# Attention scores of the first four blocks in banks of their own, and a table of held steps in the planner

## The chip, the cores and the metric

The kernel runs on one core of a Trainium2 chip. The metric is the time of one execution on the device, in microseconds (us); less is better. A core has five engines that run side by side, each through its own instructions in a fixed order: TensorE (PE, matrix products; the loads of its stationary operand are listed as PEld), VectorE (DVE), ScalarE (ACT), GpSimd (POOL) and SyncE (SP). They wait for each other by semaphores. Data come from main memory by DMA transfers, which SP, ACT and POOL issue. Products of PE land in PSUM, which has 8 banks, each 512 fp32 columns wide on 128 partitions; ACT and DVE read them from there.

## The reference

Sliding-window attention with four sink positions, then a gated feed-forward network (FFN):

```python
# q, k, v: 4 x 8 x 768 x 64 fp32; n_sink = 4, window = 128
scores = scale * np.matmul(q, k.transpose(0, 1, 3, 2))
is_sink = pos[None, :] < int(n_sink)
rel = pos[:, None] - pos[None, :]
keep = is_sink | ((rel >= 0) & (rel < int(window)))
scores = np.where(keep, scores, -1000000000.0)
a = softmax(scores)                       # over the keys
attn_out = np.matmul(a, v)                # -> x: 3072 x 512
rms = np.sqrt(np.mean(x * x, axis=-1, keepdims=True) + 1e-06)
xn = x / rms * rms_g
g = xn @ w_gate                           # 512 x 1536
out = (g * (1.0 / (1.0 + np.exp(-g))) * (xn @ w_val)) @ w_out
```

(The softmax is written out in the original.)

## The kernel before

**Blocks and groups.** The 3072 tokens are 24 blocks of 128, numbered `g`; 6 blocks make a batch `b`, and `t` is the place of a block in its batch. Four blocks make a group `G` of the FFN, six groups in all. As the window is 128 wide, the keys of block `g` are seen by the queries of blocks `g` and `g+1` alone; the sinks of a batch are handled apart (`ss`, `esk`, `vsk`).

**One block of attention.** q, k and v of a block are loaded (`load_bf16`, `load_v`, cast on the way from fp32 to bf16; block 0's q and k come as fp32 through SP with `load_f32` and are cast by DVE or ACT, `cast`). PE transposes q and k of blocks 0 to 7 (`pe_t`, L425), and DVE or ACT copies them out of PSUM (`copy_t`, L432). `scores` (L465) multiplies the keys of a block with the queries of this block and the next: for each of 4 head pairs and 2 halves, into the four banks `("s", g, u, hi)`. In a bank lie two heads, each with 256 columns: 128 for query block `g` (n = 0) and 128 for `g+1` (n = 1). ACT takes the exponential (`exps`, L513), bank by bank, into `e`. The window is cut either beforehand, by matmuls that put a bias into the banks (`mask_bias`, L447, blocks below `PE_MASKS` = 2), or afterwards by DVE (`mask_dve`, L530) or POOL (`mask_pool`, L535, from block `POOL_MASK_FROM` = 16). `av` (L549 to L566) multiplies with v, and needs the exponentials of block `g` for its own queries and those of block `g-1` for its next. Then DVE divides by the sums (`normal`, L577, L578), ACT squares (`square`, L586), DVE scales (`rms`, L593 to L610), and x is transposed, on PE below block 8 (`pe_x`, L625, `copy_x`, L631), else by DMA.

For blocks in `SPLIT` = (0, 1) the scores and exponentials run in two passes over the same four banks, first the 128 columns of n = 0 in each half, then those of n = 1. The others do both at once. So the scores of block 3 wait for q of block 4. In the last block of a batch there is no next query block: `scores_last` (L481) fills two banks. With `MERGE` = (2,) batch 2's last scores go into one PE step with the first of the next batch, and take six banks together.

**The FFN.** For each group `ffn` makes pairs of a gate product `g` and a value product `v` (`mms`, L860), 16, 8 or 8 matmuls a piece; ACT takes `tanh` (L867), DVE makes `silu` (L873) and `hidden` (L883), `project` (L893) multiplies with `wo`, ACT scales the result and SP stores it. `CHUNKS` = (4, 2, 2) cuts group 0 into four columns of one block each, with four f-tiles (128 columns of wg or wv) in one product: gate product (0, 0, 0) is that of f-tiles 0 to 3 on block 0.

**The order.** Each step is given to `Plan` with an estimated duration, what it needs and gives, a priority, and the banks it takes and drops. `Plan.run` simulates the engines: among all steps that could be next it takes the one with the smallest `(start, priority, ...)`, and the result is the order in which the program is emitted. On the chip, semaphores alone set the times; the plan sets who stands behind whom in an engine's queue. While PE would be idle, the plan places `warm` matmuls (L400, 30 of them) on zeros.

**The loads.** POOL issues the loads of `LOADS` in that order (`sw_load`, at most `DEPTH` = 8 of them under way in the plan): `q-1` is q of block 1, `qkv-2` is q, k and v of block 2, `w-2-4` is f-tiles 2 and 3 of wg and then of wv (L378), `wo-0-6` half of wo (L384). Before the first load POOL could make the identity (`make_ident`, L271) and the bias mask (`make_bias`, L277); `POOL_AT` places them behind q-1 and k-1.

**Gates.** From block `GATE_FROM` = 8 on, `gate_of` holds the scores of a block back until the FFN has come to a certain unit (a value product or a projection), `GATE_LEAD` = 14 units ahead of the block's place.

Of the kernel before, what the change touches and what calls it, by code (L numbers as in the profile page):

```python
# [26 lines left out]
class Plan:  # L27
# [2 lines left out]

    LATE = 300
    RESERVE = 8
    HOP = {"PE": 40, "ACT": 35, "DVE": 35, "POOL": 90, "SP": 60}
    START = {"PE": 800, "ACT": 800, "DVE": 1030, "POOL": 1290, "SP": 800}

# [5 lines left out]
    def op(self, ways, needs=(), gives=(), prio=0.0, takes=(), drops=(), ring=None, work=0.0,  # L43
           mode=0):
        self.ops.append(dict(
            ways=ways, needs=set(needs), gives=tuple(gives), prio=prio, takes=tuple(takes),
            drops=tuple(drops), ring=ring, work=work, mode=mode, at=len(self.ops), ready=0,
        ))

    def land(self, ring, first, work):  # L50
# [19 lines left out]
    def run(self):  # L70
# [12 lines left out]
        while left:  # L83
            first = None

            many = min(
                (o for o in cand["PE"] if len(o["takes"]) > self.RESERVE), default=None,
                key=lambda o: o["prio"],
            )
            for e, found in cand.items():  # L90
                for o in found:
                    k = len(o["takes"])
                    if k > len(self.banks):
                        continue
# [51 lines left out]
def kernel(  # L146
# [53 lines left out]
    GB_PRIO = -100000.0  # L200
    FUSE_FROM = 2
# [125 lines left out]
    def cast(name, g, copy):  # L327
        T[name, g] = ld.tile([P, H, D], BF16, name=name)
        copy(out=T[name, g], in_=T.pop(("st", name, g)))

    def load_bf16(name, src, g):
        T[name, g] = ld.tile([P, H, D], BF16, name=name)
# [10 lines left out]
    for i, name in enumerate(F32_LOADS):  # L343
        n, g, e = name[0], int(name[2:]), {"s": "SP", "a": "ACT"}[name[1]]
        src, eng = q if n == "q" else k, {"SP": nc.sync, "ACT": nc.scalar}[e]
        op({e: (430, 1000, lambda n=n, src=src, g=g, eng=eng: load_f32(n, src, g, eng))},
           (), [(n + "st", g)], -90 + i, ring="HW", work=970)
        either({"DVE": (CAST_DVE, lambda n=n, g=g: cast(n, g, nc.vector.tensor_copy)),
                "ACT": (640, lambda n=n, g=g: cast(n, g, nc.scalar.copy))},
               [(n + "st", g), "table"], [(n, g)], -99)  # L350
# [194 lines left out]
    def av(g, u):  # L545
# [7 lines left out]
        for j in range(2):  # L553
            for hi in range(2):
                h = 4 * u + 2 * j + hi
                x = 2 * hi + j
                dest = pv[:, (h - 4 * u) * VW:(h - 4 * u + 1) * VW]
                if t >= 1:
                    nc.tensor.matmul(  # L559
                        out=dest, lhsT=T["e", g - 1, u][:, x, 1, :],  # L560
                        rhs=V16[b][:, t - 1, h, :],
                        start=(t == 1), stop=False, skip_group_check=True,
                    )
                own = (T["e", g, u][:, x, 0, :] if t + 1 < NT
                       else T["el", g][:, hi * HP + 2 * u + j, :])
# [135 lines left out]
    def block_scores(g):  # L701
# [2 lines left out]
        nq = 2 if t + 1 < NT else 1  # L704
        pa = -1000.0 + 10 * g
        early = -20.0 + g if g < 2 * GB else 0.1 * g
        slots = [("s", g, u, hi) for u in range(2) for hi in range(2)]
        parts = [(0, 1), (1, 2)] if g in SPLIT else [(0, nq)]
# [50 lines left out]
    for g in range(NB):  # L759
# [8 lines left out]
            old += [("ss", b - 2, i) for i in ((2, 4) if b - 2 < 2 else (2,))]  # L768
        for n in "qk":
            if g < QK_DMA_FROM:  # L770
                pe(225, lambda n=n, g=g: pe_t(n, g), [(n, g), "ident"] + old, [(n + "p", g)],
                   pa, takes=[(n, g)])
                ways = {"DVE": (345, lambda n=n, g=g: copy_t(n, g, nc.vector.tensor_copy)),
                        "ACT": (470, lambda n=n, g=g: copy_t(n, g, nc.scalar.copy))}
# [247 lines left out]
```

## Time and profile before

| what | value |
|---|---|
| median of 7 runs | 244.95 us (244.63 to 245.48) |
| the profiled execution's own time | 244.94 us |
| its span in the trace | 243.1 us |
| mean granted clock of PE | 0.998 |
| FFN products `g` and `v` (L860), PE busy | 69.9 and 70.7 us |
| projections `o` (L893), PE busy | 63.9 us |
| scores (L465), all blocks, PE busy | 13.0 us (x176) |
| DVE masks (L530), 128x1024 | x26, mean 683 ns |
| POOL masks (L535), 128x512 | x10, mean 636 ns |
| exponentials (L513) | x88, mean 569 ns |
| DMA reads | 28.31 MB |

The span is the time from the first to the last recorded instruction; what the whole execution takes beyond it lies before and after. "Busy" is the time in which an engine worked on something; the mean of a matmul is longer than its step in a row of matmuls, because they overlap. In a line of the timeline stand start, length, engine, line of the kernel, operation, output and inputs, their sizes, how many were merged, and in brackets how long the engine had been idle before and for what it waited. In the slices of the page each digit is the busy share of one fortieth of the span in tenths.

### The profile page before, as it was taken

Reading aid. Unit: us, or ns where it says so; the run is one execution under the profiler, and the core shown is the slowest. Engines: PE = TensorE matmul, PEld = TensorE weight load, DVE = VectorE, ACT = ScalarE, POOL = GpSimd, SP = SyncE. Lnnn points to the kernel's source line nnn. Section 1 sums busy time; section 2 is a strip of 40 time slices with the busy share of each in tenths; the row PEclk is TensorE's granted clock in tenths of the full one; section 3 lists DMA queues with packets and bytes.
Section 4 is the critical chain, followed back from the end, with each engine's and each line's share of the span. In section 5 each row is a group of like instructions: output and inputs, shape, how many; then the busy total and the mean of one; then the engine's idle time right before and its main releaser. Section 6 shows DMA issues by size and latency. Waiting matters only on the chain.

```text
span 243.1 us, 5492 instructions
## 1 busy us (share of the span) xinstructions
PE 234.1 (96%) x2096; PEld 148.1 (61%) x2116; DVE 181.7 (75%) x482; ACT 130.8 (54%) x267; POOL 89.5 (37%) x116
## 2 busy tenths in 40 slices
PE   7978999999999999999999999999999999999994
PEld 3658996875788875686796544544554444444443
DVE  4479978896999998998898889895379760377700
ACT  4786465779684827575734574573553311333111
POOL 7985875596344645326511130331320000000000
PEclk9999999999999999999999999999999999999999
DMA  9999999999999999999999561110231002200022
GB/s 129 155 170 195 186 187 188 158 140 176 144 197 151 155 133 153 165 228 139 141 144 123 111 172 25 22 22 34 78 108 24 1 0 86 86 3 0 0 86 86
DMA packets 113579, 27.35 MB, mean 112 GB/s; under 512 B 103697, under 2 KB 110609, under 8 KB 113554
## 3 DMA queue, kind: packets, MB, share of 16 engines
q0 software_dynamic: 81760, 13.90, 78.8%
q1 hardware_dynamic: 31648, 12.98, 29.3%
q8 instruction: 16, 0.26, 0.5%
q10 hardware_dynamic: 146, 0.13, 0.2%
q14 instruction: 9, 0.07, 0.1%
HBM read 28.31 MB, written 6.29 MB: 142 GB/s over the span
## 4 chain that ended last, share of the span: by engine, by line
PE 78%; DMA 12%; POOL 5%; issue 1%; ACT 1%; DVE 0%; POOLq 0%
PE o L893 23%; PE v L860 23%; PE g L860 22%; DMA wv<-in_moe_w_val_dram 7%; DMA q<-in_q_dram 5%; PE s L465 3%; PE av L566 2%; PE av L559 1%; POOL v L337 1%; PE av L549 1%; PE o_last L911 1%; POOL q L333 1%; POOL wg L378 1%; POOL k L333 1%; POOL wv L378 1%
## 5 line engine op out<-in xcount | busy, mean ns | idle before, releaser
L860 PE MATMUL g<-xnt,wg 128*128 128x128 bf16 (+2 forms) x525 | 69.9, 282 | 1.2 <-DMA wg<-in_moe_w_gate_dram 1.0
L860 PE MATMUL v<-xnt,wv 128*128 128x128 bf16 (+2 forms) x524 | 70.7, 281 | 0.2
L867 ACT ACTIVATE th<-g 128x512 bf16<-128x512 f32 x72 | 43.1, 599 | 50.7 <-PE g L860 46.1
L893 PE MATMUL o<-wo,hT 128*128 128x512 bf16 x263 | 63.9, 379 | 0.8 <-issue 0.2
L873 DVE SCALAR_TENSOR_TENSOR p<-th,g 128x512 bf16<-128x512 bf16 x72 | 48.0, 682 | 21.9 <-ACT th L867 21.5
L860 PEld LDWEIGHTS <-wg 128*128 128x128 bf16 x528 | 43.2, 98 | 20.6 <-DMA wg<-in_moe_w_gate_dram 1.5
L860 PEld LDWEIGHTS <-wv 128*128 128x128 bf16 x528 | 43.0, 98 | 19.2 <-issue 0.5
L883 DVE TENSOR_TENSOR hT<-p,v 128x512 bf16<-128x512 bf16 x72 | 47.1, 680 | 1.5 <-PE v L860 0.7
L513 ACT ACTIVATE e<-s 128x512 bf16<-128x512 f32 (+1 forms) x88 | 43.9, 569 | 7.8 <-PE s L465 6.4
L893 PEld LDWEIGHTS <-hT 128*128 128x128 bf16 x276 | 25.3, 98 | 26.6 <-issue 1.5
L333 POOL DMA_DIRECT2D k<-in_k_dram x23 | 20.4, 886 | 17.8 <-DMA v<-in_v_dram 11.4
L901 ACT ACTIVATE osb<-o 128x512 f32<-128x512 f32 x23 | 13.8, 602 | 23.7 <-PE o L893 23.3
L337 POOL DMA_DIRECT2D v<-in_v_dram x24 | 21.3, 889 | 12.0 <-DMA q<-in_q_dram 9.8
L333 POOL DMA_DIRECT2D q<-in_q_dram x23 | 20.5, 891 | 10.5 <-DMA k<-in_k_dram 4.4
L578 DVE TENSOR_TENSOR x<-av,rden 128x256 bf16<-128x256 f32 x48 | 20.4, 424 | 1.6
L586 ACT ACTIVATE sq<-x 128x512 bf16<-128x512 bf16 x24 | 15.2, 631 | 11.2 <-DVE x L578 11.2
L610 DVE SCALAR_TENSOR_TENSOR xr<-x,r,gb 128x512 bf16<-128x512 bf16 x24 | 18.0, 751 | 0.9
L530 DVE TENSOR_TENSOR e<-e,masks 128x1024 bf16<-128x1024 bf16 x26 | 17.0, 683 | 1.2 <-ACT e L513 1.2
L535 POOL TENSOR_SCALAR_AFFINE_SELECT e<-e 128x512 bf16<-128x512 bf16 x10 | 6.4, 636 | 31.2 <-ACT e L513 15.7
L566 PE MATMUL av<-v,e 128*128 128x65 bf16 x192 | 17.0, 194 | 0.4 <-ACT e L513 0.4
L566 PEld LDWEIGHTS <-e 128*128 128x128 bf16 x192 | 13.0, 98 | 2.8 <-ACT e L513 0.5
L559 PE MATMUL av<-v,e 128*128 128x65 bf16 x160 | 14.5, 193 | 0.0
(75 smaller groups left out, 182.0 us busy)
## 6 DMA issues: line engine op xcount, KB each, us to landing
out_dram<-osb SPq DMA_DIRECT2D x23, 256.0 KB, 2.3
v<-in_v_dram POOLq DMA_DIRECT2D x24, 128.0 KB, 12.3
q<-in_q_dram POOLq DMA_DIRECT2D x23, 128.0 KB, 12.1
k<-in_k_dram POOLq DMA_DIRECT2D x23, 128.0 KB, 11.5
wo<-in_moe_w_out_dram POOLq DMA_DIRECT2D x2, 768.0 KB, 11.5
wg<-in_moe_w_gate_dram POOLq DMA_DIRECT2D x5, 256.0 KB, 7.9
wv<-in_moe_w_val_dram POOLq DMA_DIRECT2D x5, 256.0 KB, 8.3
stage<-in_k_dram SPq DMA_DIRECT2D x1, 256.0 KB, 3.3
```

Of the source, the lines that this page charges most:

```text
L333: nc.gpsimd.dma_start(out=T[name, g], in_=block_of(src, g))
L337: nc.gpsimd.dma_start(out=V16[b][:, t, :, 0:D], in_=block_of(v, g))
L513: nc.scalar.activation(out=T["e", g, u][:, 2 * hi:2 * hi + 2, n0:n1, :].rearrange("p x n c -> p x (n c)"), in_=ps.rearrange("p (j c) -> p ...
L530: nc.vector.tensor_tensor(out=ev, in0=ev, in1=mv, op=ALU.mult)
L566: nc.tensor.matmul(out=dest, lhsT=own, rhs=V16[b][:, t, h, :], start=(t == 0), stop=True, skip_group_check=True,)
L578: nc.vector.tensor_tensor(out=T["x16", g][:, 4 * u:4 * u + 4, :], in0=pvv[:, :, 0:D], in1=rden.unsqueeze(2).to_broadcast((P, 4, D)), op=AL ...
L610: nc.vector.scalar_tensor_tensor(out=T["xr", g], in0=T.pop(("x16", g)).rearrange("p h d -> p (h d)"), scalar=r[:, 3:4], in1=gb, op0=ALU.mu ...
L860: nc.tensor.matmul(out=ps[:, i * n:(i + 1) * n], lhsT=w_sb[:, kt, ft * P:(ft + 1) * P], rhs=T["xnt", G][:, kt, cols], start=(kt == 0), sto ...
L867: nc.scalar.activation(out=T["th", key], in_=BANK[("g", key)], func=ACT.Tanh, scale=0.5,)
L873: nc.vector.scalar_tensor_tensor(out=T["p1", key], in0=T.pop(("th", key)), scalar=1.0, in1=BANK.pop(("g", key)), op0=ALU.add, op1=ALU.mult,)
L883: nc.vector.tensor_tensor(out=T[hk][:, i:i + n, cols], in0=T.pop(("p1", key)).rearrange("p (n c) -> p n c", n=n), in1=BANK.pop(("v", key)) ...
L893: nc.tensor.matmul(out=BANK[("o", G, tb)], lhsT=T["h", G, ft // 4][:, ft % 4, tb * P:(tb + 1) * P], rhs=wo[:, ft, :], start=(ft == 0), sto ...
```

## The change

It has five parts.

1. **Own banks.** `SPLIT` is now (0, 1, 2, 3). For these blocks a new branch of `block_scores` makes, for each query block n, `bias_part` (blocks below `PE_MASKS`, which is now 3), `scores_part` and two `exps_part`, and from block 3 on `mask_part` on DVE. Each n has two banks of its own, `("s", g, n, hi)`, with the four heads of one half side by side, and one 128x512 exponential per bank. `av` reads the exponentials of such blocks from `T["ep", g, n]`.
2. **Halved casts.** The casts of block 0's q and k become two steps each, four heads a step, which DVE or ACT may take.
3. **A table of held steps.** `HOLD` gives 25 steps a number of nanoseconds, looked up by the first thing a step gives; it is added to the start in the key by which `Plan.run` chooses. The start itself is not changed.
4. **Loads and POOL.** The first weight piece stands before v-0, v-1 behind block 2, w-6-8 before w-4-6; w-8-9 and w-9-10 become w-8-10; block 6 stands before the second half of wo. The identity is made before q-1.
5. **Numbers.** `MERGE` gets batch 1 as well, `POOL_MASK_FROM` goes to 14, `GATE_FROM` to 7, `GATE_LEAD` to 12, `MASKS_PRIO` to -20.

```diff
+    HOLD = {
+        ('th', (0, 0, 0)): 200,
+        ('qT', 3): 600,
+        ('wg', 6): -600,
+        ('mb', 0, 1): -100,
+        ('e', 3, 0, 1): -600,
+        ('wv', 2): -200,
+        ('ms', 2): 900,
+        ('g', (0, 4, 256)): -600,
+        ('xr', 3): -600,
+        ('qcast', 0, 1): -900,
+        ('ms', 0): 100,
+        ('x', 2, 1, 0): 100,
+        'idnos': -900,
...
+    }
...
+            hold=self.HOLD.get(gives[0], 0) if gives else 0,
...
-                    key = (start, o["prio"], ready, o["at"])
+                    key = (start + o["hold"], o["prio"], ready, o["at"])
...
-    MASKS_PRIO = -5
-    POOL_AT = (1,2)
+    MASKS_PRIO = -20
+    POOL_AT = (0,2)
     DEPTH = 8
-    LOADS = "q-1 k-1 v-0 w-0-2 v-1 qkv-2 qkv-3 w-2-4 w-4-6 w-6-8 w-8-9 w-9-10 w-10-12 qkv-4 wo-0-6 qkv-5 wo-6-12 qkv-6 qkv-8 qkv-7"
+    LOADS = "q-1 k-1 w-0-2 v-0 qkv-2 v-1 qkv-3 w-2-4 w-6-8 w-4-6 w-8-10 w-10-12 qkv-4 wo-0-6 qkv-5 qkv-6 wo-6-12 qkv-8 qkv-7"
...
-    PE_MASKS = 2
-    POOL_MASK_FROM = 16
+    PE_MASKS = 3
+    POOL_MASK_FROM = 14
...
-    GATE_FROM = 8
+    GATE_FROM = 7
...
-    GATE_LEAD = 14
+    GATE_LEAD = 12
...
-    SPLIT = (0,1)
+    SPLIT = (0,1,2,3)
...
-    MERGE = (2,)
+    MERGE = (1,2)
...
+    def bias_part(g, n):
+        for hi in range(2):
+            nc.tensor.matmul(
+                out=bank(("s", g, n, hi)), lhsT=ident if g % NT else idnos,
+                rhs=bias[:, n:n + 1, :].to_broadcast((P, HP, P)),
+                start=True, stop=False, skip_group_check=True,
+            )
+
+    def scores_part(g, n):
+        b, t = divmod(g, NT)
+        qkT = T["qkT", b]
+        for hp in range(HP):
+            for hi in range(2):
+                pr = slice(hi * D, (hi + 1) * D)
+                nc.tensor.matmul(
+                    out=(BANK.get(("s", g, n, hi)) or bank(("s", g, n, hi)))[:, hp * P:(hp + 1) * P],
+                    lhsT=qkT[pr, 1, hp, t * P:(t + 1) * P],
+                    rhs=qkT[pr, 0, hp, (t + n) * P:(t + n + 1) * P],
+                    start=g >= PE_MASKS, stop=True, skip_group_check=True,
+                )
+
+    def mask_part(g, n, hi):
+        ev = T["ep", g, n][:, hi * HP:(hi + 1) * HP, :]
+        m = masks[:, 0 if g % NT == 0 else 1, n:n + 1, :]
+        nc.vector.tensor_tensor(
+            out=ev, in0=ev, in1=m.to_broadcast((P, HP, P)), op=ALU.mult,
+        )
+
+    def exps_part(g, n, hi):
+        if ("ep", g, n) not in T:
+            T["ep", g, n] = epool.tile([P, H, P], BF16, name=f"e{n}", bufs=3)
+        nc.scalar.activation(
+            out=T["ep", g, n][:, hi * HP:(hi + 1) * HP, :].rearrange("p x c -> p (x c)"),
+            in_=BANK.pop(("s", g, n, hi)), func=ACT.Exp, scale=inv_sqrt_d,
+        )
...
+        if g in SPLIT:
+            for n in range(2):
+                slots = [("s", g, n, hi) for hi in range(2)]
+                biased = g < PE_MASKS
+                if biased:
+                    pe(432, lambda g=g, n=n: bias_part(g, n),
+                       [("bias", n), "ident", "idnos"] + ([("qp", g + n), ("kp", g)] if g else []),
+                       [("mb", g, n)], pa + 10 * n, takes=slots)
+                pe(240, lambda g=g, n=n: scores_part(g, n),
+                   [("kT", g), ("qT", g + n)] + ([("mb", g, n)] if biased else []),
+                   [("s", g, n)] + ([("s", g)] if n else []), pa + 10 * n + 1,
+                   takes=() if biased else slots, mode=1)
+                for hi in range(2):
+                    act(480, lambda g=g, n=n, hi=hi: exps_part(g, n, hi),
...
+                    if not biased:
+                        dve(335, lambda g=g, n=n, hi=hi: mask_part(g, n, hi),
...
```

The remaining entries of the table are ('h', (0, 0, 128)): -400, ('h', (0, 4, 0)): 200, ('v', 3): -100, ('x', 3, 0, 0): 100, ('xr', 2): 200, ('th', (0, 8, 0)): 200, ('wg', 8): -600, ('q', 6): -600, ('x', 3, 0, 1): -100, ('av', 2, 0): -100, ('kT', 3): 100 and ('th', (0, 0, 256)): -400.

More of the change, by code (lines that the diff above doesn't have):

```diff
@@ L34 @@
     RESERVE = 8
+    HOLD = {
[12 more added lines that the diff above has]
+        'idnos': -900,
+        ('h', (0, 0, 128)): -400,
+        ('h', (0, 4, 0)): 200,
+        ('v', 3): -100,
+        ('x', 3, 0, 0): 100,
+        ('xr', 2): 200,
+        ('th', (0, 8, 0)): 200,
+        ('wg', 8): -600,
+        ('q', 6): -600,
+        ('x', 3, 0, 1): -100,
+        ('av', 2, 0): -100,
+        ('kT', 3): 100,
+        ('th', (0, 0, 256)): -400,
+    }
     HOP = {"PE": 40, "ACT": 35, "DVE": 35, "POOL": 90, "SP": 60}
@@ L195 @@
     WARM = 30
-    GATE_LEAD = 14
+    GATE_LEAD = 12
     T_LEAD = 4
-    SPLIT = (0,1)
+    SPLIT = (0,1,2,3)
     CHUNKS = (4,2,2)
     GB_PRIO = -100000.0
+    HALVES = ("qs0","ks0")
+    HALF = set()
     FUSE_FROM = 2
-    MERGE = (2,)
+    MERGE = (1,2)
     const = ctx.enter_context(tc.tile_pool(name="const", bufs=1))
@@ L325, in load_f32, with cast @@
         eng.dma_start(out=T["st", name, g], in_=block_of(src, g))
-    def cast(name, g, copy):
-        T[name, g] = ld.tile([P, H, D], BF16, name=name)
-        copy(out=T[name, g], in_=T.pop(("st", name, g)))
+    def cast(name, g, part, parts, copy):
+        if (name, g) not in T:
+            T[name, g] = ld.tile([P, H, D], BF16, name=name)
+        hs = slice(part * H // parts, (part + 1) * H // parts)
+        copy(out=T[name, g][:, hs, :], in_=T["st", name, g][:, hs, :])
     def load_bf16(name, src, g):
@@ L347 @@
            (), [(n + "st", g)], -90 + i, ring="HW", work=970)
-        either({"DVE": (CAST_DVE, lambda n=n, g=g: cast(n, g, nc.vector.tensor_copy)),
-                "ACT": (640, lambda n=n, g=g: cast(n, g, nc.scalar.copy))},
-               [(n + "st", g), "table"], [(n, g)], -99)
+        parts = 2 if name in HALVES else 1
+        for i in range(parts):
+            either({"DVE": (CAST_DVE // parts + 40 * (parts - 1),
+                            lambda n=n, g=g, i=i, m=parts: cast(n, g, i, m, nc.vector.tensor_copy)),
+                    "ACT": (640 if parts == 1 else 390,
+                            lambda n=n, g=g, i=i, m=parts: cast(n, g, i, m, nc.scalar.copy))},
+                   [(n + "st", g), "table"], [(n, g) if parts == 1 else (n + "cast", g, i)], -99)
+        if parts == 2:
+            HALF.add((n, g))
     op({"ACT": (430, 2100, lambda: nc.scalar.dma_start(
@@ L557, in av @@
                 dest = pv[:, (h - 4 * u) * VW:(h - 4 * u + 1) * VW]
+                y = hi * HP + 2 * u + j
                 if t >= 1:
                     nc.tensor.matmul(
-                        out=dest, lhsT=T["e", g - 1, u][:, x, 1, :],
+                        out=dest, lhsT=(T["ep", g - 1, 1][:, y, :] if g - 1 in SPLIT
+                                        else T["e", g - 1, u][:, x, 1, :]),
                         rhs=V16[b][:, t - 1, h, :],
@@ L563, in av @@
                     )
-                own = (T["e", g, u][:, x, 0, :] if t + 1 < NT
-                       else T["el", g][:, hi * HP + 2 * u + j, :])
+                own = (T["ep", g, 0][:, y, :] if g in SPLIT
+                       else T["e", g, u][:, x, 0, :] if t + 1 < NT else T["el", g][:, y, :])
                 nc.tensor.matmul(
@@ L706, in block_scores @@
         early = -20.0 + g if g < 2 * GB else 0.1 * g
+        if g in SPLIT:
[12 more added lines that the diff above has]
+                    act(480, lambda g=g, n=n, hi=hi: exps_part(g, n, hi),
+                        [("s", g, n), "table"] + ([("x", g, n, 0)] if hi else [])
+                        + ([("av", g - 2, u) for u in range(2)] if g >= 2 else []),
+                        [("x", g, n, hi)], early + n, drops=[("s", g, n, hi)])
+                    if not biased:
+                        dve(335, lambda g=g, n=n, hi=hi: mask_part(g, n, hi),
+                            [("x", g, n, hi), "masks"] + ([("e", g, n, 0)] if hi else []),
+                            [("e", g, n, hi)], early + n)
+            for u in range(2):
+                T["es", g, u] = [[("x" if biased else "e", g, n, hi) for hi in range(2)]
+                                 for n in range(2)]
+            return
         slots = [("s", g, u, hi) for u in range(2) for hi in range(2)]
-        parts = [(0, 1), (1, 2)] if g in SPLIT else [(0, nq)]
+        parts = [(0, nq)]
         if g < PE_MASKS:
@@ L770 @@
             if g < QK_DMA_FROM:
-                pe(225, lambda n=n, g=g: pe_t(n, g), [(n, g), "ident"] + old, [(n + "p", g)],
+                src = [(n + "cast", g, i) for i in range(2)] if (n, g) in HALF else [(n, g)]
+                pe(225, lambda n=n, g=g: pe_t(n, g), src + ["ident"] + old, [(n + "p", g)],
                    pa, takes=[(n, g)])
```

## The prediction

> **What bounds the kernel now.** I read the page first, for the busy shares, then the table of stretches, then the timeline of TensorE (PE) with its idle times, then that of ScalarE (ACT), and last the DMA issues with their landing times.
>
> ```profile
> span 243.1 us, 5492 instructions
> PE 234.1 (96%) x2096; PEld 148.1 (61%) x2116; DVE 181.7 (75%) x482; ACT 130.8 (54%) x267; POOL 89.5 (37%) x116
> PEclk9999999999999999999999999999999999999999
> ```
>
> The granted clock is full throughout. The stretches:
>
> ```profile
> 10.00:15.00 5.00, 4.01 (x65) 2.77 (x63) 3.81 (x16) 4.08 (x14) 5.00 (x7) 1.00 2.34 157
> 15.00:20.00 5.00, 3.41 (x49) 2.31 (x47) 4.33 (x17) 4.21 (x12) 3.34 (x6) 1.00 1.71 187
> 20.00:25.00 5.00, 5.00 (x95) 4.80 (x93) 4.56 (x13) 2.45 (x6) 3.29 (x5) 1.00 1.50 193
> 30.00:40.00 10.00, 9.53 (x163) 8.73 (x162) 8.13 (x17) 5.00 (x10) 5.93 (x8) 1.00 1.82 182
> ```
>
> After each stretch come its length, the busy time (and count) of PE, PE's weight loads, DVE, ACT and POOL, the clock, and the DMA share and GB/s. PE is full from 20 us to the last matmul near 240; what is missing after 20 us is 0.18 us at 30.3, 0.24 at 39.2, 0.16 at 55.7 and pauses of 0.05. So the end is set by how much PE work is left when PE becomes full, and only four things can move it: work done earlier than that, work removed or added, stalls after it, and the moment itself.
>
> ```profile
> 17.35 0.61 PE L465 MATMUL s<-qkT 64*128 64x256 bf16 x8
> 17.89 0.29 PE L668 MATMUL ss<-qkT,ksk 128*32 128x256 bf16 x4
> 18.12 0.28 PE L400 MATMUL warm<-zeros 128*128 128x128 bf16 x2
> 18.24 0.61 PE L860 MATMUL g<-xnt,wg 128*128 128x128 bf16 x8
> 19.70 0.62 PE L860 MATMUL g<-xnt,wg 128*128 128x128 bf16 x8 [0.84 <-DMA wg<-in_moe_w_gate_dram]
> 20.15 0.39 PE L625 MATMUL x<-ident,xr 128*128 128x128 bf16 x4
> ```
>
> That moment is 19.70: the second half of the first gate product waits for the second load of wg. It is issued at 12.24 and takes 7.4 us, so it lands at 19.65. Adding the issue and landing times of the others the same way gives v0 8.5, wg0 10.0, wv0 11.35, v1 12.5, q2 13.25, k2 14.2, v2 15.25, q3 16.05, k3 16.9, v3 17.9, wg2 19.65, wv2 20.3, wg4 21.6, wv4 23.0, wg6 24.35. They land in the order of issue, some 0.9 us apart for a block and 1.35 for a weight piece.
>
> **The change, part by part.** *The moment.* The new list has the same twelve loads ahead of the second wg load, only in another order, with the same count of POOL instructions. So I keep 19.7; bounds are 0.5 us either way (about half of one block's spacing). Making the identity first puts 0.30 us ahead of q1's issue, and the bias mask stands where it stood, behind k1.
>
> *Own banks for the first blocks.* Here is what a shared bank costs today:
>
> ```profile
> 8.27 0.38 ACT L513 ACTIVATE e<-s 128x256 bf16<-128x256 f32 x1 [0.27 <-PE s L465]
> 9.32 2.04 ACT L513 ACTIVATE e<-s 128x256 bf16<-128x256 f32 x7 [0.67 <-PE s L465]
> ```
>
> The second exponential of block 0 could follow at 8.56 and waits till 9.32, when the scores of the other query block are through (8.70 plus 0.61). Seven go by in 2.04 us, 0.28 each; the new form does the work of two in one 128x512 exponential, 0.53 each back to back (three in 1.58). Per block that is 8 x 0.28 = 2.24 against 4 x 0.53 = 2.12. Block 0's own exponentials, out near 10.7 today, come 1.5 to 2 us earlier. But v0 is now behind two weight pieces: 8.5 + 2 x 1.35 = 11.2, so av0, whose last part starts at 10.86 today, starts at 11.2. Nothing is won there; nor is it needed, because x0 is transposed at 14.71 and its first product starts at 18.24. I take 0.
>
> *What is done before 19.70.* Block 3's scores come at 33.77 now, since they take query block 4 along (0.54 us). Its first piece needs only q3 and k3 (landed 16.05, 16.9), and costs one 128-wide piece, 8 matmuls in 0.33 us (12.04 to 12.37); after 19.70 the other 0.33 is left: **-0.21**. If the first piece came too late as well, it is 0.33 + 0.33 - 0.54 = +0.12. Block 2's av stands at 21.27 to 21.98, behind a DVE mask of 1.29 us (19.66) that goes away, and q2, k2 land one place earlier (v1's, 0.9 us). Today ACT does all of block 2's exponentials between 17.78 and 20.1; half now have their scores from about 14, so the rest is out by about 18.5, and av2 can go before 19.70: **-0.71**, bounds 0 and -0.71.
>
> *What has to fit there.* Block 2's mask becomes bias matmuls: 4 of 128x512, 0.86 us (11.03 to 11.89). With the first piece of block 3 (0.33), two pieces in place of one for block 2 (0.12) and av2 (0.71) that is 2.02 us. The room between 13.5 and 19.70: idle 0.42 + 0.30 + 0.84, and 12 warm matmuls of 0.055, 2.2 us in all. It just fits, so the bias costs **0**; without that cover it costs 0.86.
>
> Could PE fall back to a slower rate while v0 is awaited? In the trace four bias matmuls take 1.89 us at 4.21 and 1.02 at 11.03; the longest PE gap between the two is 0.36, and none up to 19.70 is over 0.84. I put in nothing. The Trainium skill speaks against this: by "TensorE: Matmul & The Clock Gate", Part 1: The HAM clock gate (the "warmup" mystery), an idle window of about 3.4 us brings the array back to half rate. By it, one wait that long would cost an estimated 1.7 us (3.4 us of matmuls at half rate), and the sum would be a loss of 0.6.
>
> *After 19.70.* With av2 gone from 21.27, PE is through with two blocks' first products at 23.77 - 0.71 = 23.06. Next comes the gate product of columns 4 to 7. Its load order is turned round: 6-8 is loaded before 4-6, so column 4 lands not at 21.6 but last, at 24.35. Dry time 24.35 - 23.06 = 1.29. Against it stand av3 (0.72; at 37.23 and 38.48 today, and now it hangs on no q4) and x2, at 26.62 today, which follows an av2 that is some 2 us earlier. I take **+0.3**, bounds 0 and 1.29. An x3 long before 43.16 gives PE a fourth block of products while the last weights land, so of 0.18 + 0.24 + 0.16 = 0.58 us of stalls I take half, **-0.3**; bounds -0.58 and +0.5 (a transpose of q that comes sooner than its load, twice the 0.24).
>
> *Block 11 joined to block 12.* What a switch to scores and back costs:
>
> ```profile
> 80.21 0.40 PE L481 MATMUL s<-qkT 64*128 64x128 bf16 x8
> 80.54 1.05 PE L860 MATMUL g<-xnt,wg 128*128 128x256 bf16 x8
> ...
> 131.69 0.40 PE L481 MATMUL s<-qkT 64*128 64x128 bf16 x8
> 131.92 0.60 PE L465 MATMUL s<-qkT 64*128 64x256 bf16 x8
> ```
>
> Alone, the last block's scores take 0.33 us to the next matmul, joined 0.23; the product that follows a switch back is 0.11 longer on the chain of waits (0.98 for 0.87). 0.10 + 0.11: **-0.21**; it takes six banks at once, and if these are not free PE waits one exponential or more (0.5): bounds -0.21 and +0.5.
>
> *The rest.* Of the held steps those that could cost are the copy of q3 (600 ns back: block 2's second piece up to 0.6 later, av2 near 19.1, still in time) and the square of block 2 (900 back: x2 near 24, in the dry time above). The second half of wo stands behind three more loads, 3 x 0.9 = 2.7 us, so it lands near 31.88 + 11.5 + 2.7 = 46.1; the projections that follow 41.43 today then go behind block 3's own products: three gate and three value products of 0.89 us, 5.3 us in all for 4.7. Halved casts (0.62 whole; k's ends at 4.71, q's at 6.0) gain 0.2 to 0.3 on a chain that has v0's slack. Masks of blocks 14 and 15 go from DVE (4 x 0.65) to POOL (8 x 0.64): PE waits for neither there. Gates two units later still lie far behind: block 12 is let go by the seventh value product of group 1 (before 78 us), and its scores come at 90.42. Each 0, bounds 0.3 either way together.
>
> **Sum:** -0.21 - 0.71 + 0 + 0.3 - 0.3 - 0.21 = -1.13 us. The profiled execution took 244.94 us, 0.01 under the median of 244.95; 1.84 of it lies outside the span. 244.94 - 1.13 = 243.8.
>
> **Rivals.** *Weights pace it* (0.17): nothing fills 23.06 to 24.35, so av2 and more is given back (+1.29 for +0.3), and no stall goes. -0.21 - 0.71 + 1.29 - 0.21 = +0.16, 245.1; with av3 alone to fill half of it, 244.5. For it: PE starts on wg4 2.2 us after it lands, but on wg6 with it. Against it: av3 becomes free of q4.
>
> *v1 too late* (0.14), the slower side: v1 goes behind q2, k2, v2 and lands where v2 did, at 15.25. av1 starts at 13.60 today, so 1.7 later; if its chain of normalising, squaring and scaling stays as long as it is (14.3 to 19.7), x1 moves from 20.15 to 21.85 and the second block's products from 21.98 to 23.7. PE has nothing for 1.7 us but block 3's first piece (0.33): 1.7 - 0.33 - 0.21 = +1.16, 246.1. It decides once x1 comes over 0.7 us later than now. Against it: of these 5.4 us some 1.3 are waits behind copies and exponentials that now run at another time.
>
> *More than forecast* (0.15): dry time 0, all stalls gone and the second wg load 0.4 earlier: -0.21 - 0.71 - 0.58 - 0.21 - 0.4 = -2.1, 242.8.
>
> *It doesn't do what it says:* the held table only shifts an order, and the semaphores set the times; then only the join is left, 244.7. I count it, 0.04, with no change.
>
> **The numbers.** Forecast 0.50 at 243.8. About 0.2% (0.49 us) is what a measurement tells from no change: faster is below 244.46, slower above 245.44. Faster: 0.50 less 0.04 at its edge, 0.15, and 0.08 of the weights' case: 0.69. Same: 0.04 + 0.04, and 0.08 of the weights' case: 0.16. Slower: 0.14 and a last 0.01: 0.15. Range 242.4 to 245.4: the low end is the larger gain with the second bound of 0.4 us for unknowns; the high end leaves out the late v1.
>
> **What would show it.** Right: scores of block 3 before 19 us, av2 before the second half of the first gate product, no DVE mask of 1024 columns near 20, x3 before 30, one fewer score switch near 80 to 90. Wrong: a PE wait on wg or an x between 20 and 25 of over 0.5 us, cold matmuls after 11, a wait for banks at the joined scores. The forecast falls if PE becomes full later than 20.2 us without av2 and block 3's piece behind it.

## The result, and the profile after

The changed kernel is **slower**: 248.37 us, median of 15 runs (245.75 to 250.99), against 245.13 us for the kernel before (36 runs, 244.56 to 246.44); the ratio is 1.0088 with a 95% interval of 1.0067 to 1.011. The ratio leaves out runs more than 1.5% above the fastest run of their kernel (four of the changed kernel's), and is therefore smaller than the quotient of the two medians, 1.0132. The forecast was 243.8 us, and faster.

The profiled execution took 248.40 us. The page of the changed kernel opens with these lines (busy time of the engines, then the rows of tenths for PE and for its granted clock); below it stands PE's row of the kernel before:

```profile
span 246.3 us, 5534 instructions
PE 235.8 (96%) x2117; PEld 149.4 (61%) x2136; DVE 178.7 (73%) x480; ACT 128.6 (52%) x259; POOL 92.7 (38%) x122
PE   7699999999999999999699999999999999999994
PEclk9999999999999999999889999999999999999999
```

```profile
PE   7978999999999999999999999999999999999994
```

Behind the first slices two marks are new: a 6 in PE's row in the twentieth slice (each is 6.16 us long, so 117 to 123 us), and in the clock's row two digits of 8, in that slice and the next. The table of PE's waits (what PE waited for: us in all, times, longest) names the cause of the first one:

```profile
PE av L644 <- POOL e L611: 2.2, 1, 2.2
```

The early part shows no such loss. The stretches that the prediction showed read like this after the change (same columns):

```profile
10.00:15.00 5.00, 3.25 (x47) 2.00 (x41) 2.22 (x8) 3.45 (x9) 4.57 (x6) 1.00 2.40 156
15.00:20.00 5.00, 4.73 (x82) 3.19 (x81) 4.11 (x19) 4.57 (x11) 4.21 (x6) 1.00 1.75 185
20.00:25.00 5.00, 4.90 (x97) 4.73 (x95) 4.70 (x14) 3.53 (x8) 2.85 (x5) 1.00 1.46 198
30.00:40.00 10.00, 10.00 (x183) 9.79 (x181) 9.30 (x18) 5.49 (x11) 5.76 (x8) 1.00 1.94 177
```

PE does less from 10 to 15 us (3.25 for 4.01, it waits for v0), more from 15 to 20 (4.73 for 3.41), and it is full from 30 to 40 where 0.47 us was missing.

**Where the time goes.** PE's timeline around the new wait (start, duration, instruction; in brackets the idle time ahead of it and what ended it):

```profile
114.86 3.63 PE L997 MATMUL o<-wo,hT 128*128 128x512 bf16 x16
...
118.43 0.19 PE L636 MATMUL av<-v,e 128*128 128x65 bf16 x1
120.78 0.20 PE L644 MATMUL av<-v,e 128*128 128x65 bf16 x1 [2.15 <-POOL e L611]
...
121.00 1.24 PE L964 MATMUL g<-xnt,wg 128*128 128x256 bf16 x8
...
124.02 1.57 PE L964 MATMUL v<-xnt,wv 128*128 128x256 bf16 x8
125.42 1.04 PE L964 MATMUL g<-xnt,wg 128*128 128x256 bf16 x8
```

The second matmul of av14 waits 2.15 us. Then eight matmuls of 128x256 take 1.57 us at 124.02, where eight of the same size take 1.04 us at 125.42. The stretches of 1 us say why (the number behind POOL's is the granted clock):

```profile
121.00:122.00 1.00, 1.00 (x14) 0.84 (x11) 0.61 (x2) 0.00 (x0) 1.00 (x3) 0.85 2.27 151
122.00:123.00 1.00, 1.00 (x14) 0.83 (x12) 0.07 (x1) 0.39 (x1) 0.48 (x1) 0.50 2.45 171
123.00:124.00 1.00, 1.00 (x18) 0.94 (x17) 0.96 (x3) 0.60 (x2) 0.00 (x0) 0.50 1.25 272
124.00:125.00 1.00, 1.00 (x9) 0.75 (x7) 0.69 (x3) 0.33 (x2) 0.00 (x0) 0.50 1.55 294
125.00:126.00 1.00, 1.00 (x11) 0.85 (x10) 0.38 (x1) 0.00 (x0) 0.00 (x0) 0.94 1.11 162
```

After the wait the clock is at half for some 3.4 us: 0.15 + 0.50 + 0.50 + 0.50 + 0.06 = **1.71 us** of work lost. With the wait that is 2.15 + 1.71 = 3.9. The span grew by 3.2 (246.3 for 243.1), so the rest of the change gains about 0.7 in this execution.

**Who is late.** What PE waits for is a mask of block 14 on POOL. POOL's timeline in the changed kernel:

```profile
112.98 0.88 POOL L366 DMA_DIRECT2D q<-in_q_dram  x1 [1.11 <-DMA k<-in_k_dram]
116.00 0.87 POOL L366 DMA_DIRECT2D k<-in_k_dram  x1 [2.15 <-DMA v<-in_v_dram]
116.87 0.88 POOL L370 DMA_DIRECT2D v<-in_v_dram  x1
117.75 0.65 POOL L611 TENSOR_SCALAR_AFFINE_SELECT e<-e 128x512 bf16<-128x512 bf16 x1
...
120.09 0.63 POOL L611 TENSOR_SCALAR_AFFINE_SELECT e<-e 128x512 bf16<-128x512 bf16 x1
```

POOL also issues the loads, in program order, and the last of them wait for the landing of earlier ones. The exponentials of block 15 are through at 113.1 and those of block 14 at 117.5, but POOL sits in front of a load until 116.00 and issues loads until 117.75. Then come four masks of block 15, because the planner put them first, and block 14's first mask runs from 120.09 to 120.72 (120.09 + 0.63). PE goes on at 120.78. So the loads hold up block 15's masks, and these hold up block 14's. The trace of the kernel before had this in plain sight:

```profile
117.51 0.87 POOL L337 DMA_DIRECT2D v<-in_v_dram  x1 [0.91 <-PE av L566]
118.58 0.63 POOL L535 TENSOR_SCALAR_AFFINE_SELECT e<-e 128x512 bf16<-128x512 bf16 x1 [0.20 <-ACT e L513]
```

POOL's last load was issued at 117.51 and its first mask, for block 16, came right behind. A mask that is moved to POOL and due before 118 has to get past that row of loads.

### The profile page after: what moved, and what is told of

It is laid out like the page before. It is cut to its first block, busy times and chain, and to the rows that moved or that the text cites. A ratio compares the mean times of both kernels' runs of the same rounds, so it can differ in the third digit from the quotient of the medians.

```text
span 246.3 us, 5534 instructions
## 1 busy us (share of the span) xinstructions
PE 235.8 (96%) x2117; PEld 149.4 (61%) x2136; DVE 178.7 (73%) x480; ACT 128.6 (52%) x259; POOL 92.7 (38%) x122
## 4 chain that ended last, share of the span: by engine, by line
PE 49%; POOL 1%; issue 0%; DVE 0%
PE g L964 15%; PE v L964 15%; PE o L997 14%; PE s L541 1%; PE av L644 1%; PE o_last L1015 1%; PE av L636 1%; PE av L625 1%; POOL e L611 0%; POOL e L616 0%; PE s L557 0%; DVE last L1026 0%; PE ss L746 0%; PE vs L728 0%
## 5 line engine op out<-in xcount | busy, mean ns | idle before, releaser
L997 PEld LDWEIGHTS <-hT 128*128 128x128 bf16 x276 | 25.8, 98 | 28.1 <-issue 1.3
L589 ACT ACTIVATE e<-s 128x512 bf16<-128x512 f32 x64 | 34.1, 607 | 6.3 <-PE s L541 6.3
L611 POOL TENSOR_SCALAR_AFFINE_SELECT e<-e 128x512 bf16<-128x512 bf16 x14 | 9.3, 665 | 35.5 <-issue 21.7
L644 PE MATMUL av<-v,e 128*128 128x65 bf16 x192 | 17.5, 197 | 4.1 <-POOL e L611 2.2
L655 DVE RECIPROCAL rden<-av 128x4 f32<-128x4 f32 x48 | 8.4, 175 | 14.0 <-PE av L644 14.0
L644 PEld LDWEIGHTS <-e 128*128 128x128 bf16 x192 | 13.5, 100 | 6.4 <-POOL e L611 2.6
L636 PE MATMUL av<-v,e 128*128 128x65 bf16 x160 | 15.9, 197 | 0.0
```

The lines of the kernel that those rows point to most:

```text
L589: nc.scalar.activation(out=T["e", g, u][:, 2 * hi:2 * hi + 2, n0:n1, :].rearrange("p x n c -> p x (n c)"), in_=ps.rearrange("p (j c) -> p ...
L636: nc.tensor.matmul(out=dest, lhsT=(T["ep", g - 1, 1][:, y, :] if g - 1 in SPLIT else T["e", g - 1, u][:, x, 1, :]), rhs=V16[b][:, t - 1, h ...
L644: nc.tensor.matmul(out=dest, lhsT=own, rhs=V16[b][:, t, h, :], start=(t == 0), stop=True, skip_group_check=True,)
L997: nc.tensor.matmul(out=BANK[("o", G, tb)], lhsT=T["h", G, ft // 4][:, ft % 4, tb * P:(tb + 1) * P], rhs=wo[:, ft, :], start=(ft == 0), sto ...
```

## The experiments

Theory **M**: the masks of blocks 14 and 15 on POOL cost everything, by the wait and the half clock after it; the rest of the change gains about what was forecast. Rival **R**: the weight pieces ahead of v0, and the 1.7 us wait for v0 that they bring, are the loss or a good part of it. The expectations below call theory M "A"; their B is that the new order of the steps is at fault, whichever engine does the masks, and their C that the time is lost in the first 20 us. P is what the prediction said. Each ratio is to the kernel before, run beside it on the same chip.

**Masks only, both ways.** In e1 the changed kernel gets `POOL_MASK_FROM` back at 16, in e2 the kernel before gets 14, in e4 the changed kernel 15.

```diff
-    POOL_MASK_FROM = 14
+    POOL_MASK_FROM = 16
```

> The changed kernel with one number put back: blocks 14 and 15 are masked by DVE again (POOL_MASK_FROM 16). Theory A (the POOL queue: the masks of block 14 stand behind the last loads, PE waits 2.15 us for them at 118.6 and then runs at half clock from 121.9 to 125): the wait and the low clock go, 244.2 to 244.9 us, with little spread. Theory B (the new order of steps, from the held table, the join and the gates, puts av14 at a bad place whoever does the mask): stays at 246 to 248.5. Theory C (the first 20 us lost the time): stays at 246 to 248.5 with no wait near 118.

> The kernel before with that number alone changed (POOL_MASK_FROM 14). Theory A: the loads of the last blocks end near 118 us there too, so a PE wait on a POOL mask of 1 to 3 us appears and the time is 246 to 249 with a wide spread. Theories B and C: within 0.5 us of before.

> The changed kernel with POOL masking from block 15 (POOL_MASK_FROM 15). Theory A: four masks instead of eight stand behind the loads and the block is needed later (av15 was at 122 to 123.3), so the wait is 0 to 1 us and the clock stays full: 244.3 to 245.8. Theory B: 246 to 248.5.

Measured: e1 244.0 us, ratio 0.9957 (0.9945 to 0.997). e2 250.7 us, 1.0233 (1.0212 to 1.0253). e4 245.05 us, 1.0006 (0.9988 to 1.0024). Both sides agree with M and not with B or C: without the two blocks on POOL the change is a gain, and the two blocks alone make the kernel before slower. The sizes were off a little: e1 lies 0.2 us under its range and e2 1.7 us over its own. PE's wait and the clock in e2, whose stretches are 2 us long:

```profile
PE av L566 <- POOL e L535: 3.2, 1, 3.2
```

```profile
120.00:122.00 2.00, 1.88 (x11) 0.87 (x12) 0.61 (x2) 1.09 (x2) 2.00 (x5) 0.57 1.76 103
122.00:124.00 2.00, 2.00 (x29) 1.71 (x28) 0.92 (x4) 1.06 (x3) 0.97 (x2) 0.58 1.64 152
```

It is the same step (the second matmul of an av that waits for a mask on POOL) and the same pair: a wait of 3.2 us, then 2 x 0.43 + 2 x 0.42 = 1.70 us of clock lost. With one block on POOL (e4) the wait is 0.6 us, and the median lies 1.0 us above e1's; its profiled execution also lost clock, but early, behind the wait for v0 (see the last section). But `POOL_MASK_FROM` also enters the planner's costs, and the planner lays out the rest of the program anew. The next kernel excludes that.

**Same order, only the executing engine changed.** The planner's order is left as it is in the changed kernel; the masks of blocks 14 and 15 stand where they stood, but run on DVE.

```diff
     def mask_pool(g, u, n):
         et = T["e", g, u][:, :, n, :]
-        if n == 0:
+        if g < 16:
+            nc.vector.tensor_tensor(
+                out=et, in0=et, in1=masks[:, 1, n:n + 1, :].to_broadcast((P, 4, P)),
+                op=ALU.mult,
+            )
+        elif n == 0:
...
```

> The changed kernel with the planner left as it is, so every step keeps its place, but the eight masks of blocks 14 and 15 are carried out by DVE where POOL was. Theory A: as e1 within 0.3 us, 244.2 to 245.0. Theory B: the order is the same, so 246 to 248.5.

Measured: 243.73 us, 0.9945 (0.9933 to 0.9957). Run again later as h0, on another chip:

> e3 again (the changed kernel, all steps in their places, DVE doing the masks of blocks 14 and 15), as the base for the next two on the same chip: 0.9945 of before, within 0.002.

243.7 us, 0.9941 (0.9923 to 0.9959). So theory M holds: nothing but the engine of eight masks separates 248.4 from 243.7 us (by the ratios, 1.0088 from 0.9945), and the rest of the change gains about 0.6% (1.3 to 1.4 us by the ratios). e3 came out 0.5 us under the range expected for M.

**What makes block 14's masks late: block 15's masks or the loads?** f1 puts block 14's masks ahead of block 15's in POOL's row. f2 leaves the masks as they are and moves the last three loads (q, k, v of block 23) behind them.

```diff
# f1
+    def masks_of(g):
+        return [x for x in order if x[2] == "POOL" and x[4]["gives"]
+                and x[4]["gives"][0][:2] == ("e", g)]
+    late = masks_of(15)
+    order = [x for x in order if not any(x is y for y in late)]
+    at = max(i for i, x in enumerate(order) if any(x is y for y in masks_of(14))) + 1
+    order[at:at] = late
# f2
+    late = [x for x in order if x[2] == "POOL" and x[4]["gives"][0] in
+            (("q", 23), ("k", 23), ("v", 23))]
...
+    order[at:at] = late
```

> The changed kernel with POOL's queue alone reordered: the four masks of block 14 ahead of the four of block 15 (block 15's exponentials come first, but PE wants av14 first); the loads stay ahead of both. Theory A1 (both the loads and block 15's masks delay av14): block 14's first mask ends near 118.4, so the 2.15 us wait goes, and av15, wanted near 119.9, waits about 0.8 us for the third pair: 244.6 to 245.6 us, clock full. Theory A2 (the loads alone are the cause): little changes, 246 to 248.5.

> The changed kernel with POOL's queue alone reordered: the loads of block 23's q, k and v go behind the masks of blocks 14 and 15; the masks stay on POOL and in their order. Theory A: block 15's masks run from about 112, block 14's from 116.5, no PE wait over 0.3 us near 118: 243.7 to 244.4. If POOL's slowness with masks and not the loads were the cause: 245.5 or more.

f1 took 246.22 us, 1.0039 (1.0015 to 1.0062), and f2 244.17 us, 0.9965 (0.9944 to 0.9985); the kernel before was at 245.3 on this chip. f2 is where theory M had it; f1 is 0.6 us above the range of its theory A1, so its time alone would fit A2, and only its trace tells the two apart. In f1 block 14 no longer waits, but then block 15 does, behind it:

```profile
121.37 0.20 PE L644 MATMUL av<-v,e 128*128 128x65 bf16 x1 [0.65 <-POOL e L611]
```

In f2, POOL's timeline shows the masks as soon as their exponentials are there, and PE does not wait for POOL at all:

```profile
112.10 0.63 POOL L611 TENSOR_SCALAR_AFFINE_SELECT e<-e 128x512 bf16<-128x512 bf16 x1 [0.24 <-ACT e L589]
...
116.50 0.64 POOL L611 TENSOR_SCALAR_AFFINE_SELECT e<-e 128x512 bf16<-128x512 bf16 x1 [2.01 <-ACT e L589]
...
118.84 0.89 POOL L366 DMA_DIRECT2D q<-in_q_dram  x1
```

So the masks could stay on POOL: with the loads behind them, block 15's masks run at 112.10 and are out of the way of block 14's, and nothing waits. With the loads ahead, the order among the masks decides which block feels it. f1's wait of 0.65 us is less than its loss: 1.0039 against the 0.9945 of e3 is some 2.3 us. Its profiled execution (245.38 us, among its fastest) also waits 2.03 us for v0; the rest is not explained.

**The half clock by itself.** f3 is the changed kernel with 20 matmuls of zeros ahead of av14, about as long as the wait. They write a bank that av14 then starts anew, so the output is unchanged.

```diff
+        if (g, u) == (14, 0):
+            for _ in range(20):
+                nc.tensor.matmul(
+                    out=pv[:, 0:HW], lhsT=zeros, rhs=wo[:, 0, 0:HW], start=True, stop=True,
+                    skip_group_check=True,
+                )
```

> The changed kernel with 20 matmuls on zeros (260 columns, 0.11 us each, 2.2 us) ahead of av14, where PE waits 2.15 us; their result is overwritten. The wait is then busy. Theory H (the idle PE loses its clock: 3.4 us at half rate, 1.7 us, in most runs): the wait's 2.2 us stay but the clock is full, 245.9 to 246.6 with a spread under 1 us. Theory N (the low clock is chance, not the wait's): 246 to 251 as the changed kernel.

Measured: 247.1 us (246.04 to 248.32, 11 runs), 1.0068 (1.0041 to 1.0095). That is over the range of theory H, 245.9 to 246.6, and the spread is 2.3 us, not under 1. Its profiled execution has the filler in place of the wait, and the clock stays at 1.00 behind it:

```profile
117.72 2.38 PE L626 MATMUL av<-wo,zeros 128*128 128x260 bf16 x20
...
120.08 0.20 PE L650 MATMUL av<-v,e 128*128 128x65 bf16 x1
```

One spell of 1.71 us is 0.7% of 246 us, and so shows as a mean clock of 0.993. Nine of the 16 executions of the changed kernel (the profiled one included) have 0.993 or less (median 249.02 us) and seven have 0.997 or more (median 246.35). With the filler, two of 11 have 0.993 and nine 0.998 or more; e2, with the longest wait, has 0.993 or less in four of four. This points to the idle time as what makes the clock fall, in part of the executions. It is not proof by itself: nine of 16 against two of 11 would come about by chance some five times in a hundred, the ratios 1.0068 and 1.0088 have intervals that overlap, and a mean clock does not tell which wait lost it (f3 still waits 1.9 us for v0). The traces are the stronger evidence: in none does the recorded clock fall while matmuls are still to come, other than behind a wait of 1.6 us or more. The median is 0.4 us above 248.37 - 1.71 = 246.7, which a loss of the wait alone would give, and the two groups of the changed kernel lie 2.7 us apart, not 1.7: some 0.4 to 1.0 us of these runs is not explained.

**Parts of the change, with the masks back on DVE.** Each of these is e1 with one edit more: own banks for blocks 0 and 1 only and two biased blocks (e5), an empty table (e6), block 11 not joined (e7), v0 ahead of the first weights (e8).

```diff
# e5
-    PE_MASKS = 3
+    PE_MASKS = 2
-    SPLIT = (0,1,2,3)
+    SPLIT = (0,1)
# e6
-    HOLD = {
...
-    }
+    HOLD = {}
# e7
-    MERGE = (1,2)
+    MERGE = (2,)
# e8
-    LOADS = "q-1 k-1 w-0-2 v-0 qkv-2 ...
+    LOADS = "q-1 k-1 v-0 w-0-2 qkv-2 ...
```

> e1 (the changed kernel with POOL masks from block 16, 244.0 us) with banks of their own and bias only for blocks 0 and 1 again (SPLIT 0,1; PE_MASKS 2). Theory P (what the prediction said of the first 24 us: block 3's first piece early, av2 before the second wg load): loses 0.9 us, 244.7 to 245.1. Theory Q (these gave nothing, the gain is from the held table or the join): 243.8 to 244.3.

> e1 with an empty table of held steps. Theory P: the table only shifts an order, within 0.3 us of e1, 243.7 to 244.3. Theory Q (the table gives the gain): 244.7 or more.

> e1 with only batch 2's last scores joined to the next block's, as before. Theory P: one switch more, +0.21 us, 244.1 to 244.4. Theory Q (the join makes PE wait for six banks, or nothing at all): 243.6 to 244.0.

> e1 with v of block 0 loaded before the first weight pieces, as before the change; the rest of the new list stays. PE waits 1.2 us for v0 at 11 to 12.3 in e1. Theory P (x0 has slack, the wait costs nothing): within 0.3 us of e1. Theory R (the wait pushes x0 from 14.7 to 17.4 and sometimes drops the clock to half right after): 0.3 to 1.0 us faster than e1, 243.0 to 243.7.

Measured, with the kernel before at 245.12: e5 248.63 us, 1.0154 (1.0128 to 1.018); e6 246.73, 1.007 (1.0051 to 1.009); e7 246.53, 1.0064 (1.0041 to 1.0086); e8 246.93, 1.0084 (1.0053 to 1.0115). All four lie above every range that theory P gave, and lose more than their part was priced at, e6, e7 and e8 most of it late; of the rivals only e6's Q (the table gives the gain, 244.7 or more) has its time in its range. By the work done on PE up to 60 us (the columns of its matmuls, counted by their weight loads at 0.42 ns each, without bias and warm) e6 is 0.2 us behind e1, e8 1.0 and e5 2.2, about half of its loss; e7 is level with e1 to 0.1 even at 100 us. What decides then is shown by the waits of PE in e7:

```profile
PE g L964 <- DVE hT L987: 1.8, 1, 1.8
```

e5 has the same wait, e8 has 1.8 us for a v of a late block, e6 two of 0.7 at 150 to 170 us. In e8's profiled execution the clock also falls twice, behind a wait of 1.61 us for q2 and behind that of 1.78 for the late v. Each edit makes the planner lay out the late part anew, and a wait there is worth more than the edit. These four are inconclusive on their parts; they only show how much hangs on a late order that no one edit was about. e5 alone shows an early loss, 2.2 us by 60 us, for which the prediction had 0.9; with the planner's new order in it, it can't be put down to the banks alone. Whether e6's late loss is the table's own worth stays open.

g1 does the reverse: the kernel before with own banks for the first four blocks (the new branch of `block_scores`) and three biased blocks, and nothing else of the change.

```diff
-    PE_MASKS = 2
+    PE_MASKS = 3
-    SPLIT = (0,1)
+    SPLIT = (0,1,2,3)
```

> The kernel before with own banks for blocks 0 to 3 and the bias for block 2, and nothing else of the change (old list of loads, no held steps, old join, gates and POOL masks, whole casts). Theory P (the prediction's terms: -0.21 and -0.71, less stalls): by 60 us PE is 0.6 to 1.2 us ahead of before, and if nothing late goes wrong 243.9 to 244.6. Theory W (only the banks with the new loads together pay): within 0.4 us of before at 60 us, 244.8 or more.

245.78 us, 1.0032 (1.0006 to 1.0059): the expectation failed. By PE's work it is 1.2 us ahead of the kernel before at 60 us, as theory P had it, but 0.4 at 100, and its span is no shorter (243.1 us both); no single wait stands out, but PE is at 9.76 of 10 us at 60 to 70, 9.84 at 90 to 100 and 9.75 at 150 to 160 (before: 9.95, 9.95, 9.89). A lead in the prologue is not a lead at the end.

**Loads, with the planner kept out.** h1 and h2 are h0 with POOL's row edited after planning: h1 issues v0 ahead of the first weight pieces, h2 puts the columns 4 and 5 ahead of 6 and 7 again.

```diff
# h1
+    v0 = next(x for x in order if x[2] == "POOL" and x[4]["gives"][0] == ("v", 0))
+    order = [x for x in order if x is not v0]
+    at = next(i for i, x in enumerate(order) if x[2] == "POOL" and x[4]["gives"][0] == ("wg", 0))
+    order.insert(at, v0)
# h2
...
+    for n in ("wg", "wv"):
+        i, j = place((n, 6)), place((n, 4))
+        order[i], order[j] = order[j], order[i]
```

> h0 with one POOL instruction moved: v0's load ahead of the first two weight loads; every other instruction of every engine keeps its place (e8 had let the planner reorder everything). Theory P (v0's wait costs nothing): within 0.2 us of h0. Theory R (PE's 1.6 us wait at 12 us pushes x0 and what follows): 0.2 to 0.8 us faster than h0. If it is slower by over 0.2, the early weights carry part of the gain.

> h0 with the loads of f-tiles 4-5 and 6-7 exchanged back, every other instruction in its place. The prediction's dry time (+0.3: column 4 lands last) says 0 to 0.4 us faster than h0; if PE is never dry before f-tile 4 (theory D: av3 and x2 fill it), within 0.2 us of h0.

h1 took 244.69 us, 0.9961 (0.9945 to 0.9976), and h2 243.49 us, 0.9935 (0.9917 to 0.9953), beside h0's 243.7. In h1 the wait for v0 only moves, as PE's waits show:

```profile
PE q L464 <- DMA q<-in_q_dram: 2.1, 1, 2.1
```

v0 comes sooner, q2 later. Block 0's x is transposed at 17.51 (16.70 in h0), and the kernel is 0.5 (by the ratios, whose intervals overlap) to 1.0 us (by the medians) slower. Five of its 12 executions have a mean clock of 0.993 or less, one of h0's six has: the new wait seems to cost clock as well. **R falls**: the weights ahead of v0 are no loss against v0 first. Whether the order of the loads carries some of the gain is not settled, as the intervals overlap. h2 is the fastest version run, 0.65% or 1.6 us ahead of the kernel before; its interval overlaps h0's, so the exchange itself is worth nothing that can be told.

## Why the prediction was wrong, by its own steps

**The step that failed** is in "The rest": "Masks of blocks 14 and 15 go from DVE (4 x 0.65) to POOL (8 x 0.64): PE waits for neither there." It counts the work that is moved, and not the row that it is moved into. PE did wait, 2.15 us in the profiled execution (3.2 in e2), and the clock fell after it. By e3, undone at the same order, this one step costs 248.37 - 243.73 = 4.6 us between the medians, and 3.5 us by the ratios (1.0088 - 0.9945 of 245 us). The prediction had it at 0, within 0.3. The instructions themselves were priced rightly, 0.63 to 0.65 us each.

**No clock fall** ("I put in nothing") was argued for the wait for v0 and from rows where no gap is over 0.84 us. That is right for the kernel before and says nothing of a new gap of 2.15; and behind the wait for v0 itself the clock did fall in e4's profiled execution. The rule that was set against it (the Trainium skill, "TensorE: Matmul & The Clock Gate", Part 1: The HAM clock gate (the "warmup" mystery)) had the size right: 3.4 us at half rate, estimated at 1.7 us, and 1.71 measured. It had the condition otherwise: the idle time here was 2.15 us, 1.83 in e4 and 1.61 in e8, and not 3.4.

**The moment and what is done before it.** v0 landed at 12.2, not 11.2, and v1 at 16.0 for 15.25. PE's timeline of the changed kernel:

```profile
12.30 0.42 PE L644 MATMUL av<-v,e 128*128 128x65 bf16 x8 [1.69 <-DMA v<-in_v_dram]
17.46 0.39 PE L703 MATMUL x<-ident,xr 128*128 128x128 bf16 x4
18.34 0.79 PE L498 MATMUL s<-qkT 64*128 64x128 bf16 x16
19.42 0.28 PE L625 MATMUL av<-vsk,esk 128*128 128x260 bf16 x1
20.14 1.06 PE L964 MATMUL g<-xnt,wg 128*128 128x128 bf16 x16
21.09 0.39 PE L703 MATMUL x<-ident,xr 128*128 128x128 bf16 x4
29.05 0.39 PE L703 MATMUL x<-ident,xr 128*128 128x128 bf16 x4
```

At 18.34 stand block 2's second piece and block 3's first, at 19.42 av2: both before 20 us, as forecast. The first gate product comes whole at 20.14, where its second half came at 19.70. x3 is at 29.05, before 30 as forecast (43.16 before). x0 and x1 come later than before (14.71 and 20.15), and x1 is 0.94 later, which is beyond the 0.7 from which the case of a late v1 was to decide. It did not decide: av2, block 3's piece and av3 (22.32) filled PE. So the steps behind the terms -0.21 and -0.71 are done early, as written, but the first products come later for it: by PE's work (counted as above) the changed kernel is 0.2 us ahead of the kernel before at 20 us and 0.2 behind at 24, and h0 is 0.3 ahead at 24. Of the 0.92 booked before 19.70 no more than 0.3 is there at 24 us.

The identity, which was to go ahead of q1's load, runs behind it as before: the load starts at 1.31 us and the identity at 2.41 (1.32 and 2.42 before).

**Dry time +0.3** does not show: PE is busy 4.90 of 5 us from 20 to 25 and full from 25 to 40, and h2, with the columns back in their order, has the same 9.90 from 20 to 30. **Stalls -0.3** was too little: 0.47 us of idle time is gone between 30 and 40 alone. **The join -0.21** stays open: e7 is level with e1 at 100 us, and its end is set by another wait.

**The sum without the failed step** was -1.13 us. e1 has -1.04 (medians), e3 and h0 by their ratios -1.35 and -1.45, e3 by medians -1.31. So the sum came out at about the forecast size without the failed step, but not by its terms, and that is in part luck. By PE's work the changed kernel is 0.2 us behind the kernel before at 24 us, 0.1 ahead at 40 and 0.75 ahead at 60 and 100; h0 goes from 0.3 at 24 to 1.3 at 60. Both gain about 0.95 us by unbroken work from 24 to 60 us, where the prediction had -0.3 for stalls against +0.3 of dry time, and little before, where it had -0.92. A step priced at nothing then turned the sign.

## What to carry to other kernels

When work is moved to an engine, read that engine's timeline at the moment when the work is due, not its busy share: POOL was at 38% over the span and yet occupied by loads, or by waiting to issue them, until 117.75. Where an engine issues transfers in order, and some of them wait for an earlier landing (2.15 us at 116.00 here), everything behind them inherits that wait; move the transfers behind the work (f2), or keep the work elsewhere (e3). And a lead in the prologue, or one small edit of an ordered plan, is only worth what the last stages leave of it (g1's 1.2 us at 60 us came to nothing): look at the whole trace before giving it a price.

## What the runs showed of the hardware

A wait of PE of 1.6 to 3.2 us was enough to halve the granted clock, and the price was the same each time: 1.71 us lost after 2.15 us of idle time, 1.70 after 3.2 (e2), and 0.07 + 0.50 x 3 + 0.14 = 1.71 after 1.83 us in e4, in a quite different place:

```profile
12.00:13.00 1.00, 0.64 (x12) 0.60 (x12) 0.28 (x2) 0.00 (x0) 0.83 (x2) 0.93 2.43 155
13.00:14.00 1.00, 1.00 (x9) 0.66 (x7) 0.97 (x4) 0.23 (x1) 0.89 (x2) 0.50 2.43 155
16.00:17.00 1.00, 1.00 (x14) 0.49 (x13) 0.86 (x6) 0.90 (x3) 0.64 (x2) 0.86 1.81 184
```

In e8 a wait of 1.61 us was enough (the matmul that ended it, then a stretch of 1 us behind it):

```profile
12.77 0.55 PE L464 MATMUL q<-ident,q 128*128 128x128 bf16 x4 [1.61 <-DMA q<-in_q_dram]
13.00:14.00 1.00, 1.00 (x7) 0.47 (x5) 0.87 (x5) 0.58 (x1) 0.87 (x3) 0.50 2.42 154
```

It does not happen always, and up to about 2 us the length of the wait does not tell when. In the profiled executions the clock stayed full after 1.69 us (the changed kernel's wait for v0), 1.85 (e5), 1.94 (f3), 2.12 (h1), and 2.03 in f1:

```profile
12.27 0.42 PE L644 MATMUL av<-v,e 128*128 128x65 bf16 x8 [2.03 <-DMA v<-in_v_dram]
```

What decides it, no run here shows. Of the changed kernel's 16 executions seven show next to no loss of clock, so its runs lie in two groups, and a short wait in the midst of matmuls is to be priced at its length plus up to 1.7 us.
